# Two groups of seven half-size products for half of h, and the output's products in another order

## The chip, the cores and the metric

The kernel runs on one core of a Trainium2 chip. The metric is the device time of one execution in microseconds, the median of several runs. The engines work through their own queues in order and wait for each other by semaphores: PE (TensorE) multiplies, PEld loads its weights, DVE (VectorE) and ACT (ScalarE) read PE's results and do sums, copies, exps and gelus, POOL (GpSimd) does elementwise work, SP (SyncE) issues most DMAs.

## The reference

Efficient attention over 8 batches, 8 heads, 576 positions and 64 dimensions, followed by an MLP with exact gelu, 512 to 2048 to 512. All inputs and the output are float32; the kernel multiplies in bfloat16.

```python
q_s = softmax(q, over the head dimension)
k_s = softmax(k, over the sequence)
kv = np.einsum('bhsd,bhse->bhde', k_s, v)
x = np.einsum('bhsd,bhde->bhse', q_s, kv)      # then reshaped to (4608, 512)
h = x @ w_in                                   # (4608, 2048)
g = 0.5 * h * (1.0 + erf(h * inv_sqrt2))
out = g @ w_out                                # (4608, 512)
```

## The kernel before

The 4608 tokens are worked through in nine chunks of 512 (`M`): one per batch, numbered 0 to 7, with 512 of its 576 positions each, and chunk 8 with the remaining 64 positions of all batches. A chunk has an h stage and a y stage, and the attention of a later batch is spread over the same stages: `exp_q` and `exp_k` on ACT, `norm_q` (a DVE reduction, a DVE reciprocal and a POOL multiply), `cast_v_all` (four POOL casts), `xbar_step` (a transposing DMA from SP), `kv_step` (72 small matmuls and a DVE normalisation), and `x_all` (the next chunk's x, eight matmuls into four banks, each then copied to `xT` by ACT or DVE). All work of an engine runs in the order in which the code issues it; that order is written out by hand.

**h stage.** h is built transposed, as 16 tiles of 128 features by 512 tokens. A plain tile is four matmuls of 512 columns (`h_mm`, line 356) and one gelu on ACT (line 362) into `g`. Tiles 0 to 7 are the upper half (`UP`), 8 to 15 the lower (`DN`, written `HK` + number); the 512 tokens have a lower half (`lo`) and an upper one (`hi`). In chunks 3 to 8 `h_quad` replaces the four plain tiles 2, 3, 10 and 11 by seven half-size products of a Winograd scheme: four matmuls of 256 columns each (line 455), with sums of weights (made once, in `quad_weights`) and sums of x (four DVE operations per chunk, t1 to t4) as operands. The results of these products accumulate on each other in the PSUM banks A, Bq and C, with copies by ACT (lines 476, 483, 487) and sums by DVE (r2 and r3, line 406) in between.

**The sums for y.** The y stage multiplies g with w_out in the same seven-product form, so DVE makes sums over g first (`s_parts`): s5 (line 372), s12 (line 374), and two differences in place in g (lines 380 and 381).

**y stage** (`y_phase`, and `y_last` for chunk 8). Seven products of 16 matmuls of 256 columns each, in the order 4, 5, 1, 2, 3, 6, 7, into four banks: `bd` takes 4 and then 2 on top of it, `be` takes 5 and then 3 on top, `ba` 1 and then 7, `bb` 6. DVE copies `bd` to f after product 4 and subtracts `be` from f after product 5; ACT copies `bd` to c21 after product 2 and `be` to c12 after product 3; DVE makes c22 and c11; two sums into c22 run on POOL, and SP stores. `after(i)` marks the places at which attention work is inserted.

**Banks.** The PSUM pools rotate: `psum_h` has three banks, `psum_y` two, `psum_a` one of tag "a" and a pair of tag "a2". In the y stage `bd` and `be` are the two of `psum_y`; x's tiles 0 and 1 are the next two allocations there, so they reuse the banks of `bd` and `be`. x's tile 2 lies in `xps`, the third bank of `psum_h` in the y stage.

Of the kernel before, what the change touches and what calls it, by code (L numbers as in the profile page):

```python
# [8 lines left out]
FP32 = mybir.dt.float32  # L9
# [7 lines left out]
def kernel(  # L17
# [16 lines left out]
    nc = tc.nc  # L34
# [326 lines left out]
    def h_gelu(c, ps, t):  # L361
        nc.scalar.activation(out=st[c]["g"][:, t, :], in_=ps, func=AF.Gelu)  # L362
# [20 lines left out]
    def s_ops(c, p0, n):  # L383
        s_parts(c, p0, n, (0, 1, 2))
# [22 lines left out]

    QP = 2
    quad = {}

    def quad_weights():

        quad["r"] = [wst.tile([128, 2, HT], FP32, tag="w", name=f"r{i}") for i in range(2)]
        quad["st"] = wst.tile([128, 8, 2, HT], BF16, tag="w", name="quad_st")
        up, dn = slice(QP * 128, (QP + 2) * 128), slice((QP + HK) * 128, (QP + HK + 2) * 128)
        a11, a12 = wi_bf[:, 0:2, up], wi_bf[:, 2:4, up]
        a21, a22 = wi_bf[:, 0:2, dn], wi_bf[:, 2:4, dn]
        s1, s2, s3, s4 = (quad["st"][:, i] for i in range(4))
        tt(s1, a21, a22)
        tt(s2, s1, a11, ALU.subtract)  # L420
        tt(s3, a11, a21, ALU.subtract)
        tt(s4, a12, s2, ALU.subtract)
        t1, t2, t3, t4 = (quad["st"][:, 4 + i] for i in range(4))

        def w(src, k0=0, p=None):
            if p is None:
                return lambda k, u: src[:, k, u * 128:(u + 1) * 128]
            return lambda k, u: wi_bf[:, k0 + k, (p + u) * 128:(p + u + 1) * 128]

        quad["w"] = {  # L430
            1: w(None, 0, QP), 2: w(None, 2, QP), 3: w(s4), 4: w(None, 2, QP + HK),
            5: w(s1), 6: w(s2), 7: w(s3),
        }
        quad["x"] = {4: t4, 5: t1, 6: t2, 7: t3}

    def h_quad(c):


        h_begin(c)
        g, xT = st[c]["g"], st[c]["xT"]  # L440
        b11, b12 = xT[:, 0:2, 0:HT], xT[:, 0:2, HT:M]
        b21, b22 = xT[:, 2:4, 0:HT], xT[:, 2:4, HT:M]
        t1, t2, t3, t4 = (quad["st"][:, 4 + i] for i in range(4))
        r2, r3 = quad["r"]
        tt(t1, b12, b11, ALU.subtract)
        tt(t2, b22, t1, ALU.subtract)
        tt(t3, b22, b12, ALU.subtract)
        tt(t4, b21, t2, ALU.subtract)
        mov = dict(quad["x"])
        mov.update({1: b11, 2: b21, 3: b22})  # L450

        def mm(m, ps, first):
            for u in range(2):
                for k in range(2):
                    nc.tensor.matmul(  # L455
                        ps[:, u], quad["w"][m](k, u), mov[m][:, k],
                        start=(first and u == 0 and k == 0), stop=(k == 1), skip_group_check=True,
                    )

        def plain(t):  # L460
            ps = psum_h.tile([128, M], FP32, tag="h", name="ps")
            h_mm(c, ps, t, range(NDM))
            return ps

        def gelu(up, half, src):
            k = slice(QP, QP + 2) if up else slice(QP + HK, QP + HK + 2)
            nc.scalar.activation(out=g[:, k, half], in_=src, func=AF.Gelu)

        for t in (HK, 0, HK + 1, 1):
            h_gelu(c, plain(t), t)  # L470
        A = psum_y.tile([128, 2, HT], FP32, tag="y", name="qa")
        Bq = psum_y.tile([128, 2, HT], FP32, tag="y", name="qb")
        C = psum_a.tile([128, 2, HT], FP32, tag="a", name="qc")
        lo, hi = slice(0, HT), slice(HT, M)
        mm(1, A, True)
        nc.scalar.copy(out=C, in_=A)
        s_ops(c, 0, 2)
        mm(5, Bq, True)
        ps = plain(HK + 4)
        h_gelu(c, ps, HK + 4)  # L480
        mm(6, A, False)
        mm(2, C, False)
        nc.scalar.copy(out=r2, in_=A)
        gelu(1, lo, C)
        ps = plain(4)
        mm(7, A, False)
        nc.scalar.copy(out=r3, in_=A)  # L487
        tt(r3, r3, Bq)
        h_gelu(c, ps, 4)
        ps = plain(HK + 5)  # L490
        mm(4, A, False)
        h_gelu(c, ps, HK + 5)
        gelu(0, lo, A)
        s_ops(c, 4, 1)
        ps = plain(5)
        mm(3, Bq, False)
        tt(r2, r2, Bq)
        gelu(0, hi, r3)
        h_gelu(c, ps, 5)
        s_ops(c, 5, 1)  # L500
        ps = plain(HK + 6)
        gelu(1, hi, r2)
        h_gelu(c, ps, HK + 6)
        s_ops(c, QP, 2)
        for t in (6, HK + 7, 7):
            h_gelu(c, plain(t), t)
        for which in (0, 1, 2):
            for p in (6, 7):
                s_parts(c, p, 1, (which,))

# [56 lines left out]
    def y_phase(c, ins):  # L567
# [26 lines left out]
        def after(i):  # L594
            for fn in ins.get(i, []):
                fn()

        mm(4, bd, True)
        nc.vector.tensor_copy(out=f, in_=bd)
        after(0)  # L600
        mm(5, be, True)
        after(8)
# [7 lines left out]
        after(3)  # L610
        mm(3, be, False)
        nc.scalar.copy(out=c12, in_=two(be))
        after(4)
# [11 lines left out]
    def y_last(c):  # L625

        act, wgt = y_operands(c)
        pair = psum_a.tile([128, 2, DM], FP32, tag="a2", name="yl")  # L630
        banks = [
            (psum_y.tile([128, DM], FP32, tag="y", name="yd"),
             psum_y.tile([128, DM], FP32, tag="y", name="ye"),
             psum_h.tile([128, DM], FP32, tag="h", name="yb"),
             psum_h.tile([128, DM], FP32, tag="h", name="ya")),
            (pair[:, 0], psum_a.tile([128, DM], FP32, tag="a", name="ye"), pair[:, 1],
             psum_h.tile([128, DM], FP32, tag="h", name="ya")),
        ]
# [10 lines left out]
        for j in range(2):  # L649
            bd, be, bb, ba = (ps[:, 0:HN] for ps in banks[j])  # L650
            f = zeros32[:, j * HN:(j + 1) * HN]
# [3 lines left out]
            def mm(m, ps, first):  # L655
                for k in range(HK):
# [3 lines left out]
                    )  # L660

            mm(4, bd, True)
            nc.vector.tensor_copy(out=f, in_=bd)
            mm(5, be, True)
            tt(f, f, be, ALU.subtract)
# [5 lines left out]
            tt(c22, c22, c21, ALU.subtract)  # L671
            mm(3, be, False)
            nc.scalar.copy(out=c12, in_=be)
            both = (nc.scalar if j else nc.sync, nc.sync)
            store(0, j, HN, both)
# [247 lines left out]
    for t in range(4):  # L923
# [16 lines left out]
        1: [lambda: norm_q(2, 1, 2, nc.vector)],  # L940
        2: [lambda: cast_v_all(3), lambda: xbar_step(2), lambda: load(4)],
        3: [lambda: kv_step(2), lambda: exp_k(3)],
        4: [lambda: exp_q(3), lambda: table(AF.Gelu)],
# [10 lines left out]
    for c in range(2, B + 1):  # L954
# [8 lines left out]
        if c < 3:  # L963
            h_pairs(c, ins)
        else:
            for f in ins.get(0, []):
                f()
            h_quad(c)
        yi = {}
# [50 lines left out]
```

## Time and profile before

| what | value |
|---|---|
| median of 3 runs | 265.27 us (265.23 to 267.36) |
| the profiled execution's own time | 266.13 us |
| its span | 264.2 us |
| busy: PE, DVE, ACT, POOL | 255.5, 180.2, 176.3, 66.5 us |
| first matmul of h, chunks 2, 3, 4, 5 | 73.28, 100.72, 127.72, 154.66 us |
| first matmul of y, chunks 1, 2, 4, 8 | 58.72, 87.14, 141.14, 247.75 us |
| granted TensorE clock | 1.00 in every stretch |

The span runs from the first to the last instruction of the profiled execution; its own time has some 2 us more around it. A row of a time-ordered view has the start, the duration, the engine, the line, the operation with its tiles and shapes, and how many instructions were merged; what stands in brackets is the idle time before it and what ended it. Matmul rows overlap, since a matmul's result is there some time after the next one has been issued, so a product's cost is read from the distance of starts.

### The profile page before, as it was taken

The page shows a single profiled execution, that of the slowest core. Times are in us where ns is not written, and L with a number is a line of the kernel's source. Part 1 is how long each engine was busy: PE and PEld are TensorE (multiplying, and loading weights), DVE is VectorE, ACT ScalarE, POOL GpSimd, SP SyncE. Part 2 cuts the span into 40 slices and gives each one's busy share as a digit, 9 for nine tenths or more (in the row PEclk, how much of TensorE's full clock was granted, in tenths as well). Part 3 has the DMA queues.
Part 4 walks back from the last instruction along what each step waited for, and adds up shares of the span by engine and source line. Part 5 has one row for each costly group of instructions (what it writes and reads, how often), then busy time and mean ns, then how long its engine had stood idle before and what let it go on. Part 6 is the DMA issues. An engine that isn't in the chain of part 4 may idle for free.

```text
span 264.2 us, 5859 instructions
## 1 busy us (share of the span) xinstructions
PE 255.5 (97%) x2386; PEld 169.7 (64%) x2406; DVE 180.2 (68%) x377; ACT 176.3 (67%) x288; POOL 66.5 (25%) x61
## 2 busy tenths in 40 slices
PE   7799999999999999999999999999999999999994
PEld 3344444448844886678667866686668566866683
DVE  1877586868497898685569775856585659265852
ACT  3875986888966964896479748874785475147511
POOL 1430032003765053026304350074003500030000
PEclk9999999999999999999999999999999999999999
DMA  6999999990799006960894079708910520021023
GB/s 222 399 402 426 400 409 401 393 416 38 144 390 286 18 2 199 318 240 2 239 346 175 2 154 320 283 2 112 263 27 1 158 83 0 4 86 76 0 68 91
DMA packets 43162, 50.18 MB, mean 190 GB/s; under 512 B 20224, under 2 KB 30464, under 8 KB 42880
## 3 DMA queue, kind: packets, MB, share of 16 engines
q1 hardware_dynamic: 42656, 49.32, 55.8%
q10 hardware_dynamic: 480, 0.49, 0.7%
q8 instruction: 18, 0.29, 0.5%
q14 instruction: 8, 0.07, 0.1%
HBM read 36.70 MB, written 9.44 MB: 175 GB/s over the span
## 4 chain that ended last, share of the span: by engine, by line
PE 91%; DMA 4%; DVE 1%; issue 1%; ACT 0%; POOL 0%; ACTq 0%; SPq 0%
PE ps L356 38%; PE ya L588 9%; PE ye L588 9%; PE yd L588 9%; PE ps L531 5%; PE yb L588 5%; PE qa L455 4%; PE qb L455 2%; DMA w<-in_moe_w_in_dram 2%; DMA touch<-in_moe_w_in_dram 2%; PE kv L213 2%; PE ps L322 1%; PE ya L657 1%; PE yl L657 1%; PE qc L455 1%; PE ye L657 1%
## 5 line engine op out<-in xcount | busy, mean ns | idle before, releaser
L356 PE MATMUL ps<-xT,wi_bf 128*128 128x512 bf16 x454 | 107.0, 379 | 0.9 <-POOL wi_bf L719 0.3
L362 ACT ACTIVATE g<-ps 128x512 bf16<-128x512 f32 x118 | 68.2, 598 | 36.6 <-PE ps L356 36.3
L356 PEld LDWEIGHTS <-wi_bf 128*128 128x128 bf16 x480 | 46.8, 98 | 49.2 <-issue 1.0
L252 POOL TENSOR_TENSOR e<-e,recq 128x1024 bf16<-128x1024 bf16 (+1 forms) x10 | 27.7, 2778 | 87.1 <-DVE recq L251 50.9
L588 PEld LDWEIGHTS <-g 128*128 128x128 bf16 x448 | 43.3, 98 | 7.1 <-issue 0.4
L588 PEld LDWEIGHTS <-s 128*128 128x128 bf16 x336 | 32.9, 98 | 3.8
L176 POOL CAST v_aug<-f 128x576 bf16<-128x576 f32 x26 | 18.3, 736 | 49.8 <-DMA f<-in_v_dram 49.6
L372 DVE TENSOR_TENSOR s<-g 128x256 bf16<-128x256 bf16 (+1 forms) x46 | 16.0, 348 | 16.1 <-ACT g L362 16.1
L374 DVE TENSOR_TENSOR s<-g 128x512 bf16<-128x512 bf16 (+1 forms) x46 | 26.2, 580 | 0.0
L406 POOL TENSOR_TENSOR y_sb<-y_sb 128x512 f32<-128x512 f32 x14 | 17.8, 1269 | 30.8 <-DVE y_sb L406 28.4
L250 DVE TENSOR_REDUCE qsum<-e 128x16 f32<-128x1024 bf16 (+1 forms) x13 | 21.0, 1617 | 6.0 <-ACT e L159 6.0
L159 ACT ACTIVATE e<-f 128x512 bf16<-128x512 f32 (+1 forms) x42 | 20.5, 557 | 1.5 <-DMA f<-in_q_dram 1.3
L406 DVE TENSOR_TENSOR r<-r,qb 128x512 f32<-128x512 f32 x12 | 8.2, 687 | 13.8 <-ACT r L487 12.4
L164 ACT ACTIVATE ek<-f 128x2304 bf16<-128x2304 f32 (+1 forms) x10 | 17.2, 1728 | 0.5 <-DMA f<-in_k_dram 0.5
L380 DVE TENSOR_TENSOR g<-g 128x256 bf16<-128x256 bf16 (+1 forms) x46 | 16.7, 362 | 1.2
L406 DVE TENSOR_TENSOR y_sb<-y_sb,yb 128x512 f32<-128x512 f32 (+1 forms) x8 | 5.2, 653 | 17.9 <-PE yb L588 17.8
L381 DVE TENSOR_TENSOR g<-g 128x256 bf16<-128x256 bf16 (+1 forms) x46 | 15.9, 347 | 0.0
L406 DVE TENSOR_TENSOR y_sb<-zeros,ya 128x512 f32<-128x512 f32 (+1 forms) x18 | 11.0, 611 | 6.7 <-PE ya L588 5.2
L531 PE MATMUL ps<-wo_bf,g 128*128 128x512 bf16 x62 | 14.2, 379 | 0.1
L86 ACT ACT_TABLE_LOAD x9 | 11.5, 1283 | 3.4 <-issue 3.3
L349 ACT CAST xT<-ps 128x512 bf16<-128x512 f32 x11 | 6.3, 585 | 10.8 <-PE ps L322 8.3
L588 PE MATMUL ya<-w,g 128*128 128x256 bf16 x112 | 13.4, 273 | 0.0
(99 smaller groups left out, 336.7 us busy)
## 6 DMA issues: line engine op xcount, KB each, us to landing
out_dram<-y_sb SPq DMA_DIRECT2D x16, 512.0 KB, 4.4
f<-in_k_dram SPq DMA_DIRECT2D x6, 1152.0 KB, 9.3
f<-in_v_dram SPq DMA_DIRECT2D x6, 1152.0 KB, 11.5
f<-in_q_dram SPq DMA_DIRECT2D x6, 1024.0 KB, 7.9
w<-in_moe_w_in_dram SPq DMA_DIRECT2D x6, 512.0 KB, 8.7
f<-in_v_dram SPq DMA_DIRECT2D x8, 288.0 KB, 6.0
f<-in_q_dram SPq DMA_DIRECT2D x4, 512.0 KB, 9.2
w<-in_moe_w_out_dram SPq DMA_DIRECT2D x2, 1024.0 KB, 11.8
```

What stands on the lines that cost most here:

```text
L159: nc.scalar.activation(out=dst[:, i], in_=src[:, u], func=AF.Exp)
L164: nc.scalar.activation(out=ek[b % 2][:, i:i + n], in_=st[b]["kf"][:, i:i + n].rearrange("p x (n d) -> p x n d", n=NS), func=AF.Exp,)
L176: eng.tensor_copy(out=o, in_=i)
L250: nc.vector.reduce_sum(out=qsum, in_=eq[:, :, hs, :], axis=AX.X)
L252: eng.tensor_tensor(out=eq[:, :, hs, :], in0=eq[:, :, hs, :], in1=recq.unsqueeze(3).to_broadcast([128, J, w, D]), op=ALU.mult,)
L356: nc.tensor.matmul(ps, wi_bf[:, dm, t * 128:(t + 1) * 128], st[c]["xT"][:, dm, :], start=(dm == 0), stop=(dm == NDM - 1),)
L362: nc.scalar.activation(out=st[c]["g"][:, t, :], in_=ps, func=AF.Gelu)
L374: tt(out=s12[:, a].rearrange("p k (u m) -> p k u m", u=2), in0=g[:, a].rearrange("p k (u m) -> p k u m", u=2), in1=g[:, b, hi].unsqueeze(2 ...
L406: eng.tensor_tensor(out=out, in0=in0, in1=in1, op=op)
L455: nc.tensor.matmul(ps[:, u], quad["w"][m](k, u), mov[m][:, k], start=(first and u == 0 and k == 0), stop=(k == 1), skip_group_check=True,)
L531: nc.tensor.matmul(ps, st[c]["g"][:, t, j * 128:(j + 1) * 128], wo_bf[:, t, :], start=(t == 0), stop=(t == NDF - 1),)
L588: nc.tensor.matmul(ps[:, j * HN:(j + 1) * HN], act[m][:, k, j * 128:(j + 1) * 128], wgt[m][:, k, :], start=(first and k == 0 and j == 0), ...
```

## The change

In chunks 3 to 8 a second group of seven products, made side by side with the first, replaces the plain tiles 4, 5, 12 and 13, so that eight tiles come from products and eight are plain. The weight sums are twice as wide, and r2 and r3 are made for both groups, some copies moving to DVE. The s sums over tiles 2 to 5 and 10 to 13 are made in one piece at the end of the stage. In the y stage product 3 moves ahead of product 5 and gets a bank of its own, the later `xps`; ACT copies it to c12 at once, and DVE adds `be` (product 5 alone) to c12 after product 2. This holds for chunks 1 to 7 and for the first half of `y_last`. In chunk 1 `kv_step(2)` moves from behind product 2 to behind product 1. Its matmul code, with q the group (0 or 1) and m the product, and the hand-written order:

```diff
-        quad["r"] = [wst.tile([128, 2, HT], FP32, tag="w", name=f"r{i}") for i in range(2)]
-        quad["st"] = wst.tile([128, 8, 2, HT], BF16, tag="w", name="quad_st")
-        up, dn = slice(QP * 128, (QP + 2) * 128), slice((QP + HK) * 128, (QP + HK + 2) * 128)
+        quad["s"] = wst.tile([128, 4, 2, 512], BF16, tag="w", name="quad_s")
+        quad["t"] = wst.tile([128, 4, 2, HT], BF16, tag="w", name="quad_t")
+        quad["r"] = [wst.tile([128, 2, 2, HT], FP32, tag="w", name=f"r{i}") for i in range(2)]
+        up, dn = slice(Q0 * 128, (Q0 + 4) * 128), slice((Q0 + HK) * 128, (Q0 + HK + 4) * 128)
...
+        def mm(q, m, ps, first=False):
             for u in range(2):
                 for k in range(2):
+                    if m in plain_w:
+                        k0, t0 = plain_w[m]
+                        t = Q0 + 2 * q + t0 + u
+                        w = wi_bf[:, k0 + k, t * 128:(t + 1) * 128]
+                    else:
+                        w = quad["s"][:, sum_w[m], k, (2 * q + u) * 128:(2 * q + u + 1) * 128]
                     nc.tensor.matmul(
-                        ps[:, u], quad["w"][m](k, u), mov[m][:, k],
+                        ps[:, u], w, mov[m][:, k],
...
+        def gelu(q, up, half, src):
+            t = Q0 + 2 * q + (0 if up else HK)
+            nc.scalar.activation(out=g[:, t:t + 2, half], in_=src, func=AF.Gelu)
...
+        h_gelu(c, plain(HK), HK)
+        h_gelu(c, plain(0), 0)
+        A = [bank(psum_y, "y", "qa"), None]
+        mm(0, 1, A[0], True)
+        C = bank(psum_h, "h", "qc")
+        scopy(out=C, in_=A[0])
+        s_ops(c, 0, 1)
+        Bk = [bank(psum_y, "y", "qb"), None]
+        mm(0, 5, Bk[0], True)
+        A[1] = psum_a.tile([128, 2, M], FP32, tag="a2", name="qd")[:, 0].rearrange("p (u m) -> p u m", u=2)
+        mm(1, 1, A[1], True)
+        h_gelu(c, plain(HK + 1), HK + 1)
+        mm(0, 2, C)
+        gelu(0, 1, lo, C)
+        Bk[1] = bank(psum_a, "a", "qe")
+        mm(1, 5, Bk[1], True)
+        ps = plain(1)
+        C = bank(psum_h, "h", "qc")
+        scopy(out=C, in_=A[1])
+        h_gelu(c, ps, 1)
+        mm(1, 2, C)
+        mm(0, 6, A[0])
+        vcopy(out=r2[0], in_=A[0])
+        gelu(1, 1, lo, C)
+        mm(1, 6, A[1])
+        scopy(out=r2[1], in_=A[1])
+        s_ops(c, 1, 1)
         ps = plain(HK + 6)
+        mm(0, 7, A[0])
+        vcopy(out=r3[0], in_=A[0])
         h_gelu(c, ps, HK + 6)
+        mm(1, 7, A[1])
+        scopy(out=r3[1], in_=A[1])
+        tt(r3[0], r3[0], Bk[0])
+        ps = plain(6)
+        tt(r3[1], r3[1], Bk[1])
+        h_gelu(c, ps, 6)
+        mm(0, 4, A[0])
+        mm(1, 4, A[1])
+        gelu(0, 0, hi, r3[0])
+        gelu(0, 0, lo, A[0])
+        s_parts(c, 6, 1, (0, 1))
+        mm(0, 3, Bk[0])
+        tt(r2[0], r2[0], Bk[0])
+        mm(1, 3, Bk[1])
+        tt(r2[1], r2[1], Bk[1])
+        gelu(1, 0, lo, A[1])
+        gelu(1, 0, hi, r3[1])
+        ps = plain(HK + 7)
+        gelu(0, 1, hi, r2[0])
+        gelu(1, 1, hi, r2[1])
+        h_gelu(c, ps, HK + 7)
+        h_gelu(c, plain(7), 7)
+        s_parts(c, Q0, 4, (0,))
+        s_parts(c, 7, 1, (0,))
+        s_parts(c, Q0, 4, (1,))
+        s_parts(c, 7, 1, (1,))
+        s_parts(c, 6, 2, (2,))
+        s_parts(c, Q0, 4, (2,))
...
+        bx = st[c]["xps"]
         mm(4, bd, True)
         nc.vector.tensor_copy(out=f, in_=bd)
         after(0)
+        mm(3, bx, True)
+        nc.scalar.copy(out=c12, in_=two(bx))
         mm(5, be, True)
...
         mm(2, bd, False)
         nc.scalar.copy(out=c21, in_=two(bd))
         after(3)
-        mm(3, be, False)
-        nc.scalar.copy(out=c12, in_=two(be))
+        tt(c12, c12, two(be))
         after(4)
...
             mm(4, bd, True)
             nc.vector.tensor_copy(out=f, in_=bd)
+            if j == 0:
+                mm(3, bx[:, 0:HN], True)
+                nc.scalar.copy(out=c12, in_=bx[:, 0:HN])
             mm(5, be, True)
...
-            mm(3, be, False)
-            nc.scalar.copy(out=c12, in_=be)
+            if j == 0:
+                tt(c12, c12, be)
+            else:
+                mm(3, be, False)
+                nc.scalar.copy(out=c12, in_=be)
...
-        2: [lambda: cast_v_all(3), lambda: xbar_step(2), lambda: load(4)],
-        3: [lambda: kv_step(2), lambda: exp_k(3)],
+        2: [lambda: cast_v_all(3), lambda: xbar_step(2), lambda: load(4), lambda: kv_step(2)],
+        3: [lambda: exp_k(3)],
```

`quad_weights` is still called behind product 1 of chunk 2's y stage (`yi[2]`). The old body of `h_quad`, which the printed functions show, goes.

## The prediction

> **What bounds the kernel now.** I read the busy table first, then the chain that ended last, then the stretches of one chunk, and last the engines' own order around the places that the change touches.
>
> ```profile
> PE 255.5 (97%) x2386; PEld 169.7 (64%) x2406; DVE 180.2 (68%) x377; ACT 176.3 (67%) x288; POOL 66.5 (25%) x61
> ...
> PE 91%; DMA 4%; DVE 1%; issue 1%; ACT 0%; POOL 0%; ACTq 0%; SPq 0%
> ```
>
> PE carries 91% of the chain, so a matmul removed is time gained, and a wait put in front of a matmul is time lost. DVE and ACT have a third of the span free, but only as a mean. By stages of chunk 4 (columns: length, then busy of PE, PEld, DVE, ACT, POOL, then granted clock):
>
> ```profile
> 127.89:141.30 13.41, 13.30 (x76) 7.48 (x77) 8.98 (x24) 9.81 (x18) 0.46 (x1) 1.00 0.98 341
> 141.30:154.83 13.53, 13.53 (x194) 11.78 (x192) 10.69 (x19) 9.71 (x13) 7.89 (x7) 1.00 0.05 15
> ```
>
> The h stage is 12 plain tiles and 28 half-size matmuls back to back; in the y stage DVE already has 10.7 of 13.5 us. Now the two places where DVE and ACT come close to PE. The y stage of chunk 2, time order on DVE, POOL and PE:
>
> ```profile
> 93.86 0.35 DVE L251 RECIPROCAL recq<-qsum 128x32 f32<-128x32 f32 x1
> 94.13 0.63 DVE L406 TENSOR_TENSOR y_sb<-zeros,ya 128x512 f32<-128x512 f32 x1
> 94.68 3.57 DVE L406 TENSOR_TENSOR quad_st<-wi_bf 128x512 bf16<-128x512 bf16 x1
> ...
> 99.30 0.68 DVE L406 TENSOR_TENSOR y_sb<-y_sb,yb 128x512 f32<-128x512 f32 x1
> ...
> 94.35 3.62 POOL L252 TENSOR_TENSOR e<-e,recq 128x2048 bf16<-128x2048 bf16 x1 [8.71 <-ACT ek L164]
> ...
> 97.72 0.41 PE L322 MATMUL ps<-qT,kvc 64*64 64x512 bf16 x4
> ```
>
> The first of the four weight sums, 0.42 us elsewhere, took 3.57: it ended 0.28 after POOL's normalisation (94.35 + 3.62 = 97.97). A bf16 sum on DVE and a POOL instruction exclude each other; f32 sums with a PSUM operand (94.13, 0.63) run on. The delay cost PE nothing, since x began at 97.72 while DVE still summed. The y stage of chunk 1 on ACT:
>
> ```profile
> 65.95 0.59 ACT L609 COPY y_sb<-yd 128x512 f32<-128x512 f32 x1 [0.73 <-ACT ek L164]
> 66.43 2.13 ACT L164 ACTIVATE ek<-f 128x2304 bf16<-128x2304 f32 x1
> 68.56 0.59 ACT L612 COPY y_sb<-ye 128x512 f32<-128x512 f32 x1
> 69.05 2.19 ACT L159 ACTIVATE e<-f 128x512 bf16<-128x512 f32 x4
> 71.25 1.28 ACT L86 ACT_TABLE_LOAD   x1
> ...
> 72.66 0.57 ACT L349 CAST xT<-ps 128x512 bf16<-128x512 f32 x1
> ```
>
> From 65.95 to the xT copy that releases the next h stage ACT has no gap; the chain passes through that copy.
>
> **Products: -2.4.** A plain tile is 4 matmuls of 512 columns at 0.216 (3.45 us for 16 in the chain), a half-size one 0.109 (1.75 for 16). Per chunk 16 x 0.216 = 3.46 go and 28 x 0.109 = 3.06 come: -0.40, six times -2.4. [...]
>
> **New waits inside h: +1.6.** Let t be 0 at the stage's first matmul; an engine reads a product 0.20 after its last issue (qb issued until 137.69, the r sum at 137.88). Group b's product 2 accumulates on a copy that ACT puts into the bank that group a's product 2 has just used. Product 2a is issued until 3 x 0.864 + 4 x 0.437 = 4.34; its gelu starts at 4.59 (the gelu of tile 9 before it starts at 4.10, pitch 0.49) and ends 5.19; the copy takes 0.59 and ends 5.82; 2b is due at 4 x 0.864 + 5 x 0.437 = 5.64 and starts about 5.87, 0.05 for the signal. Wait 0.23 to 0.30 (the release between two ACT instructions isn't in this trace: 0.04 to 0.10 by DVE's), taken 0.27, six times 1.6; if ACT's order hides it, 0. The other new copies and r sums have room: the tightest, the copy before product 7a, ends 0.4 before it is due.
>
> **Gelus at the end of h: +0.95.** From tile 6 (9.99) on ACT has eight gelus in a row: 0.49, 0.52 (source in SBUF) or 0.50 each, so that of tile 15 runs 13.56 to 14.15. h ends at 13.02 + 0.23 = 13.25, and y's product 4 reads tile 15 with its eighth matmul, at 14.02: wait 0.19. Chunks 3 to 7: 0.95; between 0 and 2.
>
> **y stage, c12.** Before, product 3 accumulated on product 5 and ACT emptied the bank `ye`. Now DVE adds `ye` to c12, in its queue behind all that stands ahead. x's second tile takes this bank, so PE waits for that sum.
>
> *Chunk 2: +5.1.* Product 5 is now third. In the times of before it ends 92.54; the f sum follows at 92.58, the reduction 93.21 to 95.50, the reciprocal to 95.95, c22 95.87 to 96.50. POOL starts its normalisation 0.14 after the reciprocal, 96.09, and holds off the first weight sum until 99.71. The sums have 1024 elements now: 0.68, 0.60 apart. First 100.25, second 100.29 to 100.97, third from 100.89, fourth 101.49 to 102.17, and then c12 from 102.09 to 102.78. x's second matmul, due at 97.72, starts at 102.83: 5.1 us with PE idle. Nothing hides it: h of chunk 3 was back to back behind it.
>
> *Chunk 1: +2.05.* Products 3, 5 and 1 and then kv stand ahead of product 2, so the c21 copy starts at 68.50 instead of 65.95. Behind it on ACT stay the ek exp (2.13), the q exps (2.19) and the table (1.28); only the c12 copy (0.49 of pitch) has left that place. xT starts 72.66 + 2.55 - 0.49 = 74.7, and h of chunk 2 waits for it: kv covers until 73.22, PE starts at about 75.3 instead of 73.28.
>
> *Chunks 3 to 5: +3.3.* After the last gelu (14.65) DVE sums 5888 bf16 columns, where before it was 2304: s5 0.20, s12 of four tiles 1.12 (0.26 per 512), s12 0.34, then 0.38, 0.34, 0.60, 0.60. The yd copy, f, reduction, reciprocal and c22 follow at pitches of 0.61, 0.62, 2.31, 0.27 and 0.60; c12 runs from 22.78 to 23.47. x is due at 13.25 + 0.19 + 6 x 1.75 = 23.94: 0.5 to spare. But POOL's four casts of v fall there. In chunk 4 they stretched the last seven small sums from 1.69 (114.97 to 116.66 in chunk 3) to 3.55 (141.97 to 145.52), +1.86. That gives waits of 1.3; with casts later than the sums 0, with four full casts of 0.6, 1.75. I take 1.1, as v lands 14 to 15 us after POOL's last sums in the three chunks, which puts the casts at 1.3 to 4 us into the y stage, partly behind them. Chunk 6 has no cast and chunk 7 no reduction: 0.
>
> *Last y: +1.7.* Its second use of bank `yd` waits for the yd copy, which stands behind all eight sums on DVE:
>
> ```profile
> 250.27 0.42 DVE L663 COPY zeros<-yd 128x256 f32<-128x256 f32 x1
> ...
> 250.74 1.03 PE L657 MATMUL yd<-wo_bf,s 128*128 128x256 bf16 x8 [0.21 <-DVE zeros L663]
> ```
>
> Here PE lost 250.74 - 247.75 - 3 x 0.873 = 0.37. After: the copy runs 18.35 to 18.77 (no casts), product 2, now fifth, starts 18.82, which is 5.57 after h's end against 4 x 0.873 = 3.49: 2.08 lost, 1.7 more (this counts chunk 8's gelu wait).
>
> Sum: -2.4 + 1.6 + 0.95 + 5.1 + 2.05 + 3.3 + 1.7 = **+12.3**. The profiled run took 266.13 us, 1.93 around its span of 264.2; the span becomes 276.5, that run 278.4. The median lies 0.86 below the profiled run, so on its scale 265.27 + 12.3 = 277.6.
>
> Covered at nothing: bank moves (x, kv and the last gelu free them first), the t sums at a chunk's start (t1 is late at worst by POOL's second y_sb sum, 0.1), earlier or later stores and loads (SP's issues move with the stage).
>
> [...]
>
> **Rivals.**
> *Faster:* DVE and ACT keep up and only the products count: 265.27 - 2.4 = 262.9. It decides if c12 in chunk 2 is reached before 97.7, so the four weight sums would have to come after it or not be held off. For it: both engines are a third idle. Against: DVE's order in the changed kernel has the sums ahead of c12, and the row of 3.57. Chance 0.05.
> *The weight sums slip in before POOL:* 4 x 0.62 after c22 puts c12's end at 99.7 and x's wait at 2.0: 3.1 less, and with chunks 3 to 5 at 0, 6.4 less: 271.2. Against: before, POOL went first by 0.33. Chance 0.2, together with other partial hiding between 268.5 and 272.5.
> *DVE becomes the bound:* the casts cost 1.75 in each of chunks 3 to 5 (+2.0) and the late end of h 2.0 (+1.05): 280.6, or beyond with more waits. Chance 0.1.
> *No change,* waits of about 2 in all: 0.04.
>
> **Chances.** My sum holds 0.61 (274 to 280; by the bounds of chunks 3 to 5, -3.3 and +2.0, and of the h waits). A range of 270.5 to 281 leaves some 0.2 outside. A measurement here can tell about 1%, 2.65 us, from no change: faster 0.05, same 0.04, slower 0.91.
>
> **What would show it.** In the profile after: plain matmuls on line 356 fewer by 96, PE busy less than before; in chunk 2 a PE gap near 5 us before the second x matmul, released by the DVE sum into y_sb; about 2 us before h of chunk 2, released by ACT's xT; 0.2 to 0.3 before product 2b from ACT; some 2 us in the last y before the second `yd` group. I am wrong if the chunk 2 gap is under 2 us, or if c12's sum stands in front of the weight sums.

## The result and the profile after

The changed kernel takes 277.27 us (median of 6 runs, 275.97 to 278.81), the kernel before 265.88 beside it (265.23 to 267.36): ratio 1.0428, interval 1.038 to 1.0475. The ratios here and below leave out runs more than 1.5% above their kernel's fastest, which two runs are, both of the kernel with the groups alone. The profiled run took 278.36, with a span of 276.6.

The busy table, the row of the granted clock and the chain's shares by engine, from the page of the changed kernel:

```profile
PE 260.9 (94%) x2478; PEld 178.7 (65%) x2478; DVE 201.4 (73%) x373; ACT 179.0 (65%) x294; POOL 68.8 (25%) x61
...
PEclk9999999999999995999999999999999999999999
...
PE 59%; DMA 16%; DVE 13%; ACT 8%; issue 2%; SPq 1%; DVEq 0%
```

PE fell from 91% of the chain to 59%, and DVE and ACT together rose from 1% to 21%: waits for them are now part of what sets the end. The DMAs' rise from 4% to 16% is not the change's: all of it lies in the first 51 us, ahead of the changed code, where the chain follows loads and not PE. The 5 in the clock row marks slice 16 (about 104 to 111 us), in which PE ran at half its clock. PE's busy time rose by 5.4 us although the products cost less. Some 2.8 of that is the half clock (5.77 us busy from x of chunk 3 to h of chunk 3, 3.00 before), 1.4 lies in the first 58 us, whose code is the same, and the rest is waits in the y stages that do not show as idle time, some 2.0, less the 1.0 that the h stages gained.

The stretches of chunk 4 (h stage, y stage):

```profile
137.99:151.10 13.11, 13.11 (x90) 8.61 (x88) 10.07 (x22) 9.49 (x18) 2.27 (x2) 1.00 0.94 296
151.10:164.79 13.69, 13.69 (x193) 11.76 (x192) 11.09 (x18) 10.46 (x15) 7.26 (x6) 1.00 0.22 84
```

h is 0.30 shorter than before (13.41) and y 0.16 longer (13.53). If all chunks were like this one, the kernel would be a little faster. The loss lies elsewhere. PE's waits:

```profile
PE ps L322 <- DVE y_sb L406: 5.7, 3, 4.7
PE ps L356 <- ACT xT L349: 1.8, 1, 1.8
PE yd L680 <- DVE zeros L687: 1.7, 1, 1.7
...
PE yd L608 <- DVE zeros L620: 0.5, 2, 0.2
```

The columns are us in all, times, longest. Line 322 is x, waiting for the DVE sum that empties `ye`: 4.7 of it once, in chunk 2. In time order there (DVE, then POOL, then PE):

```profile
94.71 2.28 DVE L250 TENSOR_REDUCE qsum<-e 128x32 f32<-128x2048 bf16 x1
97.09 0.35 DVE L251 RECIPROCAL recq<-qsum 128x32 f32<-128x32 f32 x1
97.36 0.63 DVE L406 TENSOR_TENSOR y_sb<-zeros,ya 128x512 f32<-128x512 f32 x1
97.91 3.84 DVE L406 TENSOR_TENSOR quad_s<-wi_bf 128x1024 bf16<-128x1024 bf16 x1
101.78 0.69 DVE L406 TENSOR_TENSOR quad_s<-quad_s,wi_bf 128x1024 bf16<-128x1024 bf16 x1
...
103.59 0.68 DVE L406 TENSOR_TENSOR y_sb<-y_sb,ye 128x512 f32<-128x512 f32 x1
...
97.58 3.62 POOL L252 TENSOR_TENSOR e<-e,recq 128x2048 bf16<-128x2048 bf16 x1 [11.22 <-ACT y_sb L623]
...
99.24 0.40 PE L322 MATMUL ps<-qT,kvc 64*64 64x512 bf16 x1
104.33 0.64 PE L322 MATMUL ps<-qT,kvc 64*64 64x512 bf16 x3 [4.69 <-DVE y_sb L406]
...
106.31 3.59 PE L608 MATMUL ya<-w,g 128*128 128x256 bf16 x16
```

POOL's multiply begins 0.33 before the first weight sum and holds it up until it has ended itself (101.20; the sum ends 0.55 later): 3.84 us for a sum that takes 0.69 in the next row. The c12 sum (103.59) stands behind all four, and x's second matmul behind it: 104.33 - 99.24 = 5.09. The last row is the part that no earlier trace had: product 7 takes 3.59 instead of 1.91, at half clock. On ACT in chunk 1:

```profile
68.08 0.59 ACT L632 COPY y_sb<-yd 128x512 f32<-128x512 f32 x1 [2.88 <-issue]
68.56 2.13 ACT L164 ACTIVATE ek<-f 128x2304 bf16<-128x2304 f32 x1
70.59 2.18 ACT L159 ACTIVATE e<-f 128x512 bf16<-128x512 f32 x4
72.78 1.28 ACT L86 ACT_TABLE_LOAD   x1
...
74.18 0.57 ACT L349 CAST xT<-ps 128x512 bf16<-128x512 f32 x1
```

ACT idles 2.88 us for product 2, which now stands behind product 3 and kv, and then has the same chain to do but for the c12 copy: xT comes at 74.18 instead of 72.66.

Set against the prediction's terms, by the distance of the stages' first matmuls, and for the last y up to the end of the span (after minus before, profiled runs):

| stretch | predicted | measured |
|---|---|---|
| start to y of chunk 1 | 0 | -0.49 |
| y of chunk 1 to h of chunk 2 | +2.05 | +2.01 |
| x of chunk 3 (in chunk 2) to h of chunk 3 | +5.1 | +7.46 |
| h of chunks 3 to 8: products and waits inside | -2.4 + 1.6 | -1.69 |
| y of chunks 3, 4, 5 | 3 x (1.1 + 0.19) | +1.46, +0.17, +1.46 |
| y of chunks 6, 7 | 2 x 0.19 | +0.17, +0.15 |
| last y | +1.7 | +1.70 |
| sum | +12.3 | +12.4 |

### The profile page after: what moved, and what is told of

Read it like the earlier page. It is cut to its first block, busy times and chain, and to the rows that moved or that the text cites. A ratio compares the mean times of both kernels' runs of the same rounds, so it can differ in the third digit from the quotient of the medians.

```text
span 276.6 us, 6029 instructions
## 1 busy us (share of the span) xinstructions
PE 260.9 (94%) x2478; PEld 178.7 (65%) x2478; DVE 201.4 (73%) x373; ACT 179.0 (65%) x294; POOL 68.8 (25%) x61
## 4 chain that ended last, share of the span: by engine, by line
PE 59%; DMA 16%; DVE 13%; ACT 8%; issue 2%; SPq 1%; DVEq 0%
PE ps L356 21%; PE ya L608 7%; DMA f<-in_k_dram 6%; PE yd L608 5%; DMA f<-in_v_dram 4%; DMA w<-in_moe_w_out_dram 4%; PE qd L451 3%; PE qa L451 3%; PE yx L608 3%; PE ye L608 3%; DMA w<-in_moe_w_in_dram 3%; DVE qsum L250 2%; DVE s L374 2%; ACT g L463 2%; PE qc L451 2%
## 5 line engine op out<-in xcount | busy, mean ns | idle before, releaser
L356 PE MATMUL ps<-xT,wi_bf 128*128 128x512 bf16 x376 | 88.7, 379 | 2.0 <-ACT xT L349 1.8
L362 ACT ACTIVATE g<-ps 128x512 bf16<-128x512 f32 x94 | 54.1, 601 | 39.0 <-PE ps L356 39.0
L356 PEld LDWEIGHTS <-wi_bf 128*128 128x128 bf16 x384 | 37.5, 98 | 39.9 <-issue 3.1
L176 POOL CAST v_aug<-f 128x576 bf16<-128x576 f32 x26 | 20.5, 819 | 54.4 <-DMA f<-in_v_dram 54.2
L372 DVE TENSOR_TENSOR s<-g 128x256 bf16<-128x256 bf16 (+2 forms) x40 | 14.9, 373 | 17.2 <-ACT g L362 17.2
L374 DVE TENSOR_TENSOR s<-g 128x512 bf16<-128x512 bf16 (+2 forms) x40 | 24.0, 611 | 0.0
L451 PEld LDWEIGHTS <-quad_s 128*128 128x128 bf16 x192 | 18.8, 98 | 3.5
L451 PEld LDWEIGHTS <-wi_bf 128*128 128x128 bf16 x144 | 14.1, 98 | 7.3 <-issue 1.3
L380 DVE TENSOR_TENSOR g<-g 128x256 bf16<-128x256 bf16 (+2 forms) x34 | 15.3, 451 | 1.0
L493 DVE COPY r<-qa 128x512 f32<-128x512 f32 x6 | 4.1, 691 | 16.0 <-PE qa L451 16.0
L608 PE MATMUL ya<-w,g 128*128 128x256 bf16 x112 | 15.1, 294 | 0.0
L381 DVE TENSOR_TENSOR g<-g 128x256 bf16<-128x256 bf16 (+2 forms) x34 | 15.0, 441 | 0.0
## 6 DMA issues: line engine op xcount, KB each, us to landing
w<-in_moe_w_out_dram SPq DMA_DIRECT2D x2, 1024.0 KB, 11.5
```

The source lines that it names most:

```text
L176: eng.tensor_copy(out=o, in_=i)
L356: nc.tensor.matmul(ps, wi_bf[:, dm, t * 128:(t + 1) * 128], st[c]["xT"][:, dm, :], start=(dm == 0), stop=(dm == NDM - 1),)
L374: tt(out=s12[:, a].rearrange("p k (u m) -> p k u m", u=2), in0=g[:, a].rearrange("p k (u m) -> p k u m", u=2), in1=g[:, b, hi].unsqueeze(2 ...
L380: tt(out=g[:, a, hi], in0=g[:, a, hi], in1=g[:, a, lo], op=ALU.subtract)
L451: nc.tensor.matmul(ps[:, u], w, mov[m][:, k], start=(first and u == 0 and k == 0), stop=(k == 1), skip_group_check=True,)
L608: nc.tensor.matmul(ps[:, j * HN:(j + 1) * HN], act[m][:, k, j * 128:(j + 1) * 128], wgt[m][:, k, :], start=(first and k == 0 and j == 0), ...
```

## The experiments

In all experiment kernels a plain DMA copy of the same 512 KB stands in place of the transposing DMA of q (so x is not the reference's); the first two runs measure what that costs. Stage lengths from the profiled runs, in us ("c1" is y of chunk 1 to h of chunk 2, "x" is the stretch from x of chunk 3 to h of chunk 3, h3 to h8 are summed, "last y" runs to the end of the span, which is known to 0.1):

| kernel | c1 | h2 | x | h3 to h8 | y3 | y4 | y5 | last y | median |
|---|---|---|---|---|---|---|---|---|---|
| before, with the copy | 14.55 | 13.86 | 3.00 | 80.50 | 13.58 | 13.53 | 13.53 | 16.41 | 265.78 |
| changed, with the copy | 16.57 | 13.86 | 9.86 | 78.68 | 14.80 | 13.71 | 14.99 | 18.14 | 277.17 |
| groups only | 14.55 | 13.86 | 3.38 | 79.83 | 15.87 | 15.01 | 15.81 | 19.03 | 277.42 |
| order only | 16.56 | 15.55 | 8.59 | 80.58 | 13.58 | 13.53 | 13.53 | 16.91 | 274.86 |
| sums in h2 | 16.57 | 15.55 | 3.01 | 78.68 | 13.76 | 14.17 | 15.06 | 18.12 | 270.54 |
| exp_k first | 14.56 | 13.86 | 10.46 | 78.88 | 14.93 | 13.71 | 14.98 | 18.07 | 275.62 |
| sums before norm | 16.57 | 15.50 | 4.92 | 78.70 | 14.23 | 13.69 | 14.98 | 18.15 | 273.76 |
| last copy on ACT | 16.57 | 13.87 | 9.54 | 78.68 | 15.05 | 13.71 | 15.11 | 17.03 | 277.24 |
| gelu 15 first | 16.56 | 13.87 | 10.46 | 79.11 | 14.55 | 13.52 | 14.49 | 18.09 | 275.92 |
| reduction late | 16.57 | 13.87 | 9.84 | 79.73 | 14.12 | 13.68 | 13.69 | 18.12 | 276.25 |
| five edits | 14.55 | 13.87 | 3.01 | 79.92 | 13.58 | 13.53 | 13.58 | 17.00 | 265.40 |
| in halves | 14.55 | 13.86 | 3.00 | 78.68 | 13.58 | 13.69 | 13.53 | 16.82 | 264.18 |

**The two bases.**

```diff
-        nc.sync.dma_start_transpose(
-            out=st[b]["qT"].rearrange("p j x m -> p (j x) m"),
+        nc.sync.dma_start(
+            out=st[b]["qT"].rearrange("p j x m -> p (j x m)"),
```

> The kernel before the change with one thing other: the transposing DMA of q (seven per run) is a plain DMA of the same 512 KB, from the same place in SP's queue to the same tile, so that x and all behind it aren't the reference's. It is the base of the experiments, which all have this copy. Expected to be within 0.5 us of the kernel before, since the transposes land a chunk ahead of their use.

> The changed kernel with the same plain copy in place of the transposing DMA. Expected to show the changed kernel's holes: 1.8 us before h of chunk 2, about 5 before x's second matmul in chunk 2 with half a clock behind it, 1.7 in the last y; 11 to 12 us above the base of before.

Measured: 265.78 (ratio 0.9999, 0.9987 to 1.0011) and 277.17 (1.0422, 1.0402 to 1.0442). The copy changes nothing in either that the whole time can show, so the other kernels may be set beside these two.

**Weight sums in the h stage of chunk 2,** away from POOL's multiply and from c12:

```diff
+            ins[4] = [quad_weights]
...
-        if c == 2:
-            yi[2] = [quad_weights]
```

> On the changed kernel with the copy: the four wide weight sums are issued in the middle of chunk 2's h stage instead of behind product 1 of its y stage. Theory (the c12 sum stood behind them on DVE, and they stood behind POOL's normalisation): the hole of 5 us before x's second matmul goes, and with it the stretch at a granted clock of 0.5 behind it (2.4 us); the sums cost 0 to 0.5 in h of chunk 2. 7.5 us less than the changed base, between 6.5 and 8. Rival (x would wait for the c12 sum anyway, because the reduction ahead of it is late): 2 us less at most, and the half clock stays.

Measured: 270.54 (1.0172, 1.0136 to 1.0209), 6.6 below the changed kernel; the stretch "x" is back at 3.01. So the weight sums ahead of c12 made the hole and the half clock behind it: 6.85 of the 11.5 us by which the two profiled bases differ. The casts of v now land elsewhere against DVE's sums, and y3 and y4 changed places as the late ones (13.76 and 14.17). One row did not fit, PE's first matmuls of chunk 2's h stage:

```profile
74.77 15.71 PE L356 MATMUL ps<-xT,wi_bf 128*128 128x512 bf16 x62 [2.06 <-ACT xT L349]
```

These matmuls took 14.03 in the changed kernel with the copy, after the same wait of 2.06; here 15.71, since half clock follows the wait (see the last section).

**exp_k(3) ahead of product 2,** so that ACT works through its exps while PE does kv:

```diff
-        2: [lambda: cast_v_all(3), lambda: xbar_step(2), lambda: load(4), lambda: kv_step(2)],
-        3: [lambda: exp_k(3)],
+        2: [lambda: cast_v_all(3), lambda: xbar_step(2), lambda: load(4), lambda: kv_step(2), lambda: exp_k(3)],
```

> On the changed kernel with the copy: only the ek exp of chunk 3 moves on ACT from behind the c21 copy of chunk 1 to ahead of it. Theory (ACT without a gap from the c21 copy to xT holds up h of chunk 2): h of chunk 2 starts 1.5 to 2.0 us earlier and the whole is as much shorter. Rival (kv or the transposed q is what h of chunk 2 waits for): no more than 0.3 us.

Measured: 275.62 (1.035, 1.0319 to 1.0381), 1.55 less; c1 is 14.56, the 2.01 are gone. That xT stood behind ACT's chain is shown.

**The groups alone, and the order alone.** The first keeps the two groups and takes the y stages and kv's place of before; the second keeps one group and takes the new ones.

```diff
# groups only (against the changed kernel)
-        mm(3, bx, True)
-        nc.scalar.copy(out=c12, in_=two(bx))
...
-        tt(c12, c12, two(be))
+        mm(3, be, False)
+        nc.scalar.copy(out=c12, in_=two(be))
...
-        2: [lambda: cast_v_all(3), lambda: xbar_step(2), lambda: load(4), lambda: kv_step(2)],
-        3: [lambda: exp_k(3)],
+        2: [lambda: cast_v_all(3), lambda: xbar_step(2), lambda: load(4)],
+        3: [lambda: kv_step(2), lambda: exp_k(3)],
```

> Two groups in h as in the changed kernel; y stages, y_last and kv's place as in the kernel before; transposing DMA replaced by a plain copy of the same bytes, as in both base runs (265.78 and 277.17). Theory: the products give what the stage accounts of the change showed, 6 x 0.3 = -1.8 in h, and -0.5 at the start. Product 2 is fourth again and waits for the yd copy, which stands behind DVE's longer sums: about 2 in chunks 3 and 5 (where the change itself, with product 2 fifth, still waited 0.38), 0.5 in chunks 4, 6 and 7, about 2.6 in the last y; chunk 2's y stage loses 0.5 to 1.5 to the wider weight sums, but no 5 us, since nobody waits for a c12 sum. Sum 273, range 270 to 275. Rival, that the new order of y alone costs the time and the products are free: 263 to 265.

> The kernel before with only y's new order, the c12 sum on DVE and kv's new place; one group of seven products; plain copy in place of the transposing DMA. Theory: chunk 1 loses 2.0 (xT behind ACT's chain), chunk 2 loses the hole before x's second matmul, about 3.9 here because the weight sums are half as wide (0.42 instead of 0.68 each), with 0 to 2.4 of half clock behind it; chunks 3 to 7 lose nothing, since DVE's sums are as short as before; the last y gains 0.4 (product 2 one place later than the yd copy needs). 265.8 + 5.5 = 271.3, to 274 with the half clock; granted clock 0.99 in the second case, 1.00 in the first. Rival, that only two groups make the order cost anything: 265 to 267.

Measured: groups only 275.36 and 275.08, both at a mean granted clock of 0.997 (ratio 1.0353, 1.0326 to 1.038), and 279.5 and 279.9 at 0.988 and 0.979. Order only 274.86 (1.0337, 1.0307 to 1.0366). Both parts cost 9 us alone, and the two rivals that made one of them free fall. The groups alone wait for the yd copy behind DVE's longer sums:

```profile
PE yd L608 <- DVE zeros L619: 5.6, 5, 2.0
```

That is y3 +2.3, y4 +1.5, y5 +2.3 and the last y +2.6, where I expected 2, 0.5, 2 and 2.6; the range of 270 to 275 missed by 0.1 to 0.4. The order alone loses only in chunks 1 and 2, and a little at the end: +0.5, though PE itself gained 0.35. From the start of the last product to the end it takes 5.55 instead of 4.70, and the trace shows SP's stores there: one issue takes 1.54 (at 267.10) where others take 0.47 to 0.75, the four behind it go out with hardly a gap, and the last store lands at 272.82, 4.57 after that start instead of 3.78. Its 274.86 lies 0.9 above the expected range, since half clock came behind both holes (h2 is 1.7 longer) and this end was not foreseen. So the new order shortens the groups' waits in y3 to y5 and the last y, by 4 us in all by the table's rows, and pays for it in chunks 1 and 2. In the order-only kernel both holes were followed by half clock; the stretches around the first (columns as above, the clock third from the end):

```profile
72.00:76.00 4.00, 1.94 (x84) 1.26 (x77) 3.86 (x8) 3.47 (x6) 1.49 (x3) 0.98 1.04 384
76.00:79.00 3.00, 2.78 (x7) 1.03 (x7) 1.04 (x2) 1.19 (x2) 3.00 (x2) 0.50 1.04 397
```

PE idled for 2 us of the first stretch, worked for 1, and then ran at half clock through the whole second.

**Weight sums ahead of the reduction,** still in chunk 2's y stage:

```diff
-            yi[2] = [quad_weights]
+            yi[1] = [quad_weights] + yi[1]
```

> The changed kernel (with the plain copy, 277.17) with one call moved: chunk 2's weight sums stand ahead of the reduction of norm_q, so POOL's multiply comes after them. Theory: the four sums take 4 x 0.62 = 2.5 instead of 5.8, the hole before x's second matmul falls from 5.1 to about 1.8, and with it goes half clock of up to 2.4: 271.5 to 274; the first weight sum lasts 0.68, not 3.8. Rival, that POOL's multiply then collides with other bf16 work on DVE (c12, y_sb or the g sums of the next stage) and the hole stays: 276 to 278.

Measured: 273.76 (1.029, 1.0264 to 1.0317). The stretch "x" is 4.92, 1.9 longer than in the kernel before, as expected (PE idle for 1.53), and no half clock follows there; but h2 took 15.50 here, so 1.6 of the gain went to half clock behind chunk 1's hole.

**The last yd copy on ACT.**

```diff
-            nc.vector.tensor_copy(out=f, in_=bd)
+            (nc.vector.tensor_copy if j else nc.scalar.copy)(out=f, in_=bd)
```

> The changed kernel (plain copy, 277.17) with the first yd copy of the last y stage on ACT instead of DVE. Theory: PE's wait of 1.7 us before the second group on yd goes, the copy then waits for nothing but product 4 and ACT's last gelu; f's subtraction on DVE stays behind the sums: -0.7 to -1.7, 275.5 to 276.5. Rival, that PE waits the same time elsewhere in the last stage (for f or be): 277.2, within 0.3.

Measured: 277.24 (1.043, 1.0394 to 1.0466), no change that the whole time can show; the last y alone is 1.1 shorter, 17.03. The wait before the second `yd` is gone and a smaller one stands before product 7, for a sum on DVE:

```profile
264.22 1.03 PE L680 MATMUL ya<-w,g 128*128 128x256 bf16 x8 [0.58 <-DVE y_sb L406]
```

1.71 became 0.58. Its time does not confirm the 1.1: the median lies where the rival had it, and the runs spread over 2.1 us.

**Tile 15's gelu first,** and the differences in one piece:

```diff
+        h_gelu(c, ps, HK + 7)
         gelu(0, 1, hi, r2[0])
         gelu(1, 1, hi, r2[1])
-        h_gelu(c, ps, HK + 7)
...
-        s_parts(c, 6, 2, (2,))
-        s_parts(c, Q0, 4, (2,))
+        s_parts(c, Q0, 6, (2,))
```

> The changed kernel (with the plain copy, 277.17) with the gelu of tile 15 ahead of the last two product gelus, and the differences over tiles 2 to 7 and 10 to 15 in two DVE instructions instead of four. Theory: product 4 of y no longer waits 0.17 to 0.19 for tile 15 in chunks 3 to 7 (-0.9 in all), and DVE's sums end 0.2 to 0.3 earlier where product 2 and x wait for DVE (chunks 3 and 5, last y): -0.2 to -1.0 more; 275.2 to 276.1, the stages of y 3 and 5 at 14.3 to 14.7 instead of 14.8 to 15.0. Rival, that the two late product gelus now hold up the sums by as much as tile 15's gelu did: the same time, within 0.4.

Measured: 275.92 (1.0373, 1.0346 to 1.04), 1.25 less. y4 falls by 0.19 to what it was before the change, y3 by 0.25, y5 by 0.50: product 4's wait was the late gelu, in every chunk. How much of the 0.50 in y5 comes from the differences in one piece, this run does not separate.

**The reduction behind c12,** in chunks 3 to 6:

```diff
-            yi[1] = [lambda nb=nb: norm_q(nb)]
+            yi[1 if c == 2 else 4] = [lambda nb=nb: norm_q(nb)]
```

> The changed kernel (plain copy, 277.17) with the reduction, reciprocal and POOL multiply of norm_q issued behind the c12 sum in chunks 3 to 6 (chunk 2 as it is). Theory: in chunks 3 and 5 the c12 sum that x's second matmul waits for stands 2.6 us nearer on DVE (reduction 2.28, reciprocal 0.3), and nothing of that wait is left; what remains of the 1.46 and 1.33 us is the wait of product 4 (0.17) and that of product 2 for the yd copy behind the sums (0.15 to 0.4): the y stages of chunks 3 and 5 fall from 14.80 and 14.99 to 13.8 to 14.2, chunk 4 stays near 13.7; -1.7 to -2.2 us, 275.0 to 275.5 but for the width of the half clock in chunk 2. Rival: POOL's multiply, now some 2 us later, holds off the t sums of the next h stage or its sums into c22, and h waits instead: 277 to 279.

Measured: 276.25 (1.0399, 1.0377 to 1.0421), 0.92 less, half of what I expected. y3 and y5 fell as said, to 14.12 and 13.69; but h4 and h7 grew by 0.14 and h5 and h6 by 0.38. The time-ordered view of that kernel at the start of h in chunks 4 and 5 (DVE, POOL, PE):

```profile
137.71 1.24 DVE L406 TENSOR_TENSOR quad_t<-xT 128x512 bf16<-128x512 bf16 x1
139.05 1.30 DVE L406 TENSOR_TENSOR quad_t<-xT,quad_t 128x512 bf16<-128x512 bf16 x1
...
135.05 3.62 POOL L252 TENSOR_TENSOR e<-e,recq 128x2048 bf16<-128x2048 bf16 x1 [7.08 <-ACT xT L349]
138.63 2.85 POOL L406 TENSOR_TENSOR y_sb<-y_sb 128x512 f32<-128x512 f32 x2
...
166.17 0.60 PE L451 MATMUL qb<-quad_t,quad_s 128*128 128x256 bf16 x4 [0.21 <-DVE quad_t L406]
```

The later multiply, until 138.67, holds off the first t sum (1.24, where a t sum alone takes 0.42), POOL's two sums pushed behind it the second (1.30), and in chunk 5, where the last row is from, product 5 waits for t1. The theory and its rival both hold here, each for a part.

**Five edits at once:** sums in h2, exp_k first, gelu 15 first, last copy on ACT, and the late reduction in chunks 3 and 5 alone.

> The changed kernel (plain copy, 277.17) with five edits at once: weight sums in the h stage of chunk 2, exp_k(3) ahead of the c21 copy in chunk 1, tile 15's gelu first with merged differences, the last yd copy on ACT, and norm_q behind the c12 sum in chunks 3 and 5 alone. Theory, against the kernel before with the copy (span 264.2): h gives 6 x 0.3 = -1.8 and the start 0 to -0.5; chunks 1 and 2 lose nothing, so there is no hole over 1 us and the clock stays at 1.00; y of chunks 3 and 5 loses 0.1 each, the h stages behind them 0.14 and 0.38 (t sums behind POOL's multiply), the last y 0.5. Sum -0.3 to -1.2: 264.6 to 265.5 us, ratio 0.995 to 0.999. Rival, that the waits only move to places that the single edits did not show: 267 or more.

Measured: 265.40 (11 runs, 265.23 to 265.99) against 265.74, ratio 0.9987 (0.9976 to 0.9997). No hole is left in chunks 1 and 2, the clock holds at 0.998 to 1.00, and every y stage but the last is within 0.05 of what it was before the change. What is left over: h4 and h6 at 13.71, the t sums again, which cost 0.6 each and not the 0.14 and 0.38 that I carried over from the kernel before this one.

**The reduction in halves,** and in the last y product 4 of the second half before product 7 of the first (against the kernel of five edits):

```diff
-            yi[4 if c in (3, 5) else 1] = [lambda nb=nb: norm_q(nb)]
+            if c in (3, 5):
+                yi[2] = [lambda nb=nb: norm_q(nb, 0, 2)]
+                yi[4] = [lambda nb=nb: norm_q(nb, 1, 2)]
+            else:
+                yi[1] = [lambda nb=nb: norm_q(nb)]
...
-            mm(4, bd, True)
+            if j == 0:
+                mm(4, bd, True)
...
+            if j == 0:
+                mm(4, banks[1][0][:, 0:HN], True, 1)
             mm(7, ba, False)
```

> As the kernel with five edits (265.40 against 265.74 for the kernel before in the same call, both with their own q transfer), but in chunks 3 and 5 norm_q goes in two halves, one ahead of product 2's copy and one behind the c12 sum, and in the last y product 4 of the second half goes ahead of product 7 of the first. Theory: the first half of the reduction (1.14) falls into the 0.8 us for which DVE waited for ACT's c12 copy, POOL's multiply ends some 2 us earlier and no longer holds off the t sums: h of chunks 4 and 6 go from 13.71 back to 13.11 to 13.2 (-1.0 to -1.2 in all), with 0 to 0.4 lost before x's second matmul; the last y loses its wait of 0.57 before product 7. Sum -0.9 to -1.8: 263.6 to 264.5 us, ratio to before 0.992 to 0.996. Rival, that the halves delay the c12 sum by their own length and x waits: 265.2 to 266.

Measured: 264.18 (264.13 to 264.85) against 265.65, ratio 0.9941 (0.9919 to 0.9962): 0.6% faster than the kernel before, with the change's two groups and its order of y. DVE and POOL in its chunk 3:

```profile
120.87 0.69 DVE L406 TENSOR_TENSOR y_sb<-zeros,ya 128x512 f32<-128x512 f32 x1 [0.27 <-PE ya L607]
121.47 1.21 DVE L250 TENSOR_REDUCE qsum<-e 128x16 f32<-128x1024 bf16 x1
122.72 0.25 DVE L251 RECIPROCAL recq<-qsum 128x16 f32<-128x16 f32 x1
122.89 0.63 DVE L406 TENSOR_TENSOR y_sb<-y_sb,ye 128x512 f32<-128x512 f32 x1
...
128.01 0.42 DVE L406 TENSOR_TENSOR quad_t<-xT 128x512 bf16<-128x512 bf16 x1
...
123.11 3.80 POOL L252 TENSOR_TENSOR e<-e,recq 128x1024 bf16<-128x1024 bf16 x2 [2.16 <-ACT y_sb L622]
```

The first half of the reduction fills time in which DVE had nothing else to do, c12 (122.89) is early enough for x at 124.20, and the multiply ends at 126.91, before t1, which is back at 0.42. h3 to h8 sum to 78.68: all that the products bring, 1.82 against the base. y4 is 0.16 longer than before: in that chunk the reduction is still in one piece, and x's second matmul waits for the c12 sum, which ends 0.13 after x's start:

```profile
147.21 2.28 DVE L250 TENSOR_REDUCE qsum<-e 128x32 f32<-128x2048 bf16 x1
...
150.34 0.68 DVE L406 TENSOR_TENSOR y_sb<-y_sb,ye 128x512 f32<-128x512 f32 x1
...
150.89 0.58 PE L322 MATMUL ps<-qT,kvc 64*64 64x512 bf16 x4
```

In the last y PE loses its wait of 0.57 before product 7 and starts its last product 0.73 sooner after the stage's start, but the stage is only 0.1 to 0.2 shorter: SP's last stores now go out one right behind the other, and the last lands 4.39 after that product's start instead of 3.78.

## Why the prediction was right

The time, the sign and the two largest causes were right: 277.6 predicted, 277.27 measured. The agreement of the sum is in part luck: one term was 2.4 us too small, and h, the start and chunks 3 to 5 were 0.5 to 0.9 too large. The profiled spans differ by 12.4, as the sum of 12.3 says; the medians of the same measurement differ by 11.4, for the kernel before had 265.88 there and not 265.27.

- **Products and the waits inside h:** the sign was right, the size not: -0.8 predicted, -1.69 measured (-1.82 undisturbed). The step "the release between two ACT instructions isn't in this trace: 0.04 to 0.10 by DVE's" was mis-sized. In the trace after, the gelu that empties a bank starts at 169.39 for 0.60, the copy into it at 169.88, one ACT pitch later and before the gelu's recorded end of 169.99. Product 2b starts at 170.53 against a due time of 169.57 + 0.864 = 170.43: 0.10, not 0.27. An exchange of 0.40 per chunk less 0.10 gives the 0.30 that each h stage shows.
- **Late gelu of tile 15:** 0.19 predicted; 0.15 to 0.17 in chunks 4, 6 and 7, and shown by the run that puts it first.
- **Chunk 2's hole:** 5.1 predicted, 5.09 measured, and shown by moving the sums. The term missed what follows it: 2.4 us of half clock. The prediction's sum has nothing for it: the trace of before, from which it was added up, has no such hole. By the trace after, the clock fell to 0.50 inside the hole, at 103.14, and rose at 109.97:

```profile
99.00:105.00 6.00, 1.31 (x15) 0.61 (x16) 5.83 (x6) 0.00 (x0) 2.25 (x2) 0.85 0.00 0
105.00:110.00 5.00, 5.00 (x92) 3.71 (x84) 1.95 (x5) 1.07 (x2) 2.49 (x2) 0.50 0.73 210
```

  That is 6.83 us, and 5.6 of them, after PE had started again, did half their work: 2.8 by this estimate, of which the stage accounts show 2.4 in the stretch and 0.1 in h of chunk 3. This is the term that made up for what the others overstated.
- **Chunk 1:** 2.05 predicted, 2.01 measured, shown by exp_k first.
- **Chunks 3 to 5:** 1.1 in each predicted, 1.29, 0 and 1.29 beside the gelu's wait. The two cases named, casts beside the sums and casts behind them, both came, in different chunks. The changed kernel's DVE and POOL in chunks 3 and 4:

```profile
124.54 2.49 DVE L374 TENSOR_TENSOR s<-g 128x2048 bf16<-128x2048 bf16 x2
...
124.35 4.01 POOL L176 CAST v_aug<-f 128x576 bf16<-128x576 f32 x4 [16.78 <-DMA f<-in_v_dram]
...
152.69 1.55 DVE L374 TENSOR_TENSOR s<-g 128x2048 bf16<-128x2048 bf16 x2
...
155.77 2.83 POOL L176 CAST v_aug<-f 128x576 bf16<-128x576 f32 x4 [15.43 <-DMA f<-in_v_dram]
```

  In chunk 3 v lands 1.4 us into the y stage, and cast and sum stretch each other (2.49 for 1.55). In chunk 4 it lands 4.7 us into it, when the sums are nearly done. A mean over the three was the wrong shape for a term that is either there or not.
- **Last y:** 1.7 predicted and measured. The run with the copy on ACT supports its cause by its stage and wait, not by its whole time.
- **The start:** -0.49 is no effect of the change. Over all profiled runs, whose starts have the same code, y of chunk 1 begins between 58.19 and 58.77.
- **What would show it:** plain matmuls did fall by 96 and the waits stand where they were said to be. "PE busy less than before" failed, for half by the half clock; in the kernel of five edits, without it, PE is busy 253.9.

The rivals: in chunk 2 POOL again went first by 0.33, so "the weight sums slip in before POOL" did not happen; made by hand (sums before norm), it gave 273.76 and not 271.2, since chunks 3 to 5 kept most of their waits (y3 14.23, y5 14.98) and h of chunk 2 lost 1.6 at half clock.

## What to carry to other kernels

An instruction that frees a bank must be priced by all that stands ahead of it in its engine's queue, and its engine may have time to spare on average: here 5 us of hole came from four sums of 0.7, the first of them held up for 3 by POOL, on an engine that was busy 73%. When PE is the bound, count a hole at its length plus the half clock that may follow it: here 1.6 to 2.5 us behind holes of 2.05 to 5.1 us, or nothing. An order that moves waits is worth trying only with its new waits removed one by one; no single edit took away more than 6.6 of the 11.4 us, and the six together turned 4.3% slower into 0.6% faster.

## What was not expected of the hardware

**Half clock after a hole of only 2.1 us.** In three profiled runs (sums in h2, order only, sums before norm) the hole of 2.05 to 2.1 us ahead of h in chunk 2 was followed by 3.41 us at 0.50; in five others (both of the changed kernel, last copy on ACT, gelu 15 first, reduction late) a hole of 1.8 to 2.1 at the same place was not. In the sums-in-h2 kernel two of four runs kept 1.00 and took 269.5 and 270.3, the profiled one had 0.994 and took 271.7. The longer hole was followed by half clock in every profile that had it, for one stretch of 3.41 us or for two (6.83), beginning between 1.9 and 5 us after the hole's start.

In the changed kernel's trace the clock's fall and rise around the long hole, at 103.14 and 109.97, lie 28 and 30 times 3.413 us after its first rise (7.57). In stretches of that length, counted from the first rise on, PE was idle for all 3.41 us of the one before the fall (99.73 to 103.14), as far as the profile's matmul rows tell it; in every other one at full clock it was idle for at most 1.84 (72.42 to 75.84, which holds the hole of chunk 1), and full clock followed. Of the two at half clock, the first had 1.18 idle, and half clock followed, the second none, and full clock followed. Stretches of 3.41 us in other profiles, four around the hole in chunk 1 and one in the long hole (start and end, length, PE's busy time; the clock third from the end):

```profile
72.69:76.10 3.41, 1.30 (x7) 0.61 (x7) 3.27 (x7) 2.64 (x6) 0.99 (x2) 1.00 1.03 389
72.83:76.25 3.42, 1.50 (x7) 0.67 (x7) 3.28 (x6) 2.67 (x5) 1.00 (x2) 1.00 1.04 398
70.98:74.39 3.41, 1.83 (x86) 1.38 (x84) 2.75 (x6) 3.38 (x7) 2.18 (x2) 1.00 1.05 365
74.39:77.80 3.41, 2.87 (x13) 1.33 (x14) 2.36 (x4) 2.20 (x5) 2.13 (x2) 1.00 1.04 412
98.55:101.96 3.41, 1.46 (x12) 0.88 (x10) 3.41 (x1) 0.01 (x1) 3.02 (x1) 1.00 0.00 0
```

The first is of sums in h2: the whole hole lies in one stretch (2.11 idle), and half clock follows. The second, of gelu 15 first, has 1.92 idle, and none follows. The next two are of the changed kernel with the copy: its hole is as long, but a stretch ends in it (1.58 and 0.54 idle), and none follows. The last, of reduction late, has 1.95 idle, and half clock follows. So a wait of 2.06 to 2.07 us for xT cost 1.6 us more in the first of these profiles and nothing in the other two that show the hole of chunk 1. That this turns on how the hole lies against such stretches is the author's estimate from these few rows; no run moved a hole against them to show it. One stretch at half clock takes about 0.5 x 3.4 / 275 = 0.006 off the mean clock: the changed kernel's runs show about 0.994 or 0.988, by this estimate one stretch or two, and the 1.7 us (0.5 x 3.41) that a stretch costs are a good part of their spread of 2.8 us.
